# First mixture: its first two token blocks go through group 0 in two halves, fewer float64 pieces before it, and the decayed values on ScalarE

## The chip, the cores and the metric

The kernel runs on one core of a Trainium2 chip. The metric is device time in microseconds; the median of three runs of the kernel before is 2010.84 us.

The engines are named as in the profile: PE (TensorE's matmuls; PEld its weight loads), DVE (VectorE), ACT (ScalarE), POOL (GpSimd) and SP (SyncE, which issues nearly all DMAs). Each works through its own queue in program order.

## The reference, cut to what matters

```python
# retention: 4 batches x 8 heads, 576 tokens, 64 values a head
scores = scale * np.matmul(q, k.transpose(0, 1, 3, 2))
ret = scores * Dmat[None, :, :, :]          # decay gamma ** (i - j), lower triangle
x = np.matmul(ret, v)                       # -> 2304 tokens x 512

# first mixture, weights in float64: 512 -> 2048 -> 512
h = x @ w_in
g = h * (1.0 / (1.0 + np.exp(-1.702 * h)))
x = (g @ w_out).astype(np.float32)

# second mixture, eight experts, weights by a Sinkhorn iteration
for e in range(E):
    ye = np.maximum(x @ w1[e], 0.0) @ w2[e]
    out += P[:, e:e + 1] * ye
```

## The kernel before, in words

Program order is written out by hand (`manual_schedule`), so the order of calls below is the order in every engine's queue.

**Products.** Every factor of the two mixtures is kept as a high and a low part (`xh`, `xl`; `wh`, `wl`), and a product is three matmuls: high by high, high by low, low by high.

**Attention** (lines 171 to 407). Heads go two at a time: 4 head pairs by 4 batches are 16 pairs p. The 576 tokens of a pair are four chunks of 128 and a rest of 64. A loop over p = 0 to 16 works on pair p and finishes pair p - 1. SP loads `kq` (line 198, three buffers) and `aux`, the values and keys by token (line 203, four buffers), two pairs ahead. PE computes `scores` (L235, L253), DVE multiplies them by the decay (`ret`, L240, L262). `state` multiplies decayed values by keys chunk after chunk in one PSUM bank (L273); ACT copies the running sum after each chunk (L281), and the next chunk's matmuls wait for that copy. `within` (L301) and `carried` (L310) build the output; ACT (L322) and DVE (L323) evict it as `xh` and `xl`. `prep_pair` makes, a pair ahead, the decayed values `vs` (L216) and decayed queries `qs` (L223), on POOL but for the first two pairs; `qs` waits for the last `carried` of the pair whose buffer it takes, so it starts at the end of an iteration.

**Float64 pieces.** The first mixture has four groups of 512 hidden columns (`FG`). A group's weights come in 16 pieces of 128 rows by 256 columns (`HW`): 4 row chunks of `w_in` by two column halves, then 4 row chunks of `w_out` by two halves. A piece has three steps:

- `load_piece`, called by `ask`: a DMA of 256 KB from SP (L112) into one of three `raw` buffers.
- `read_piece`, called by `read`: six DVE operations (L135, L139, L140, L143, L146, L147) take the float64 bits apart into a float32 value `ca` and a rest `cs` (two buffers of each). `read` holds back two pieces that are in flight.
- `split_piece`, called by `split`: ACT writes the high part (L160), POOL subtracts it (L164) and adds the rest (L165).

`prepare` is split, ask, read, of up to three different pieces. In the attention's loop every iteration asks for one piece at its begin, splits in its middle (behind `within` 0 and 1, ahead of `state` 1) and reads at its end; after the loop what is left of group 0 is prepared at once.

**First mixture** (lines 410 to 812). 2304 tokens are blocks of 512, 512, 512, 512 and 256. For each group g and block: four calls of `mm1_chunk`, one for 128 hidden columns (12 matmuls, L429; Sigmoid on ACT, L438; product on DVE, L439; high part `gh` on ACT, L440; low part `gl` on POOL, L441; two buffers `sg`), then `mm2_first` (48 matmuls, L454, four for each f at three products each). Behind each f a hook calls `prepare` for the next group's pieces: four times in blocks 0 to 2, twice in blocks 3 and 4, 16 times a group. The result goes to `acc`: copied by ACT in group 0 (L465), added by DVE in the others (L467). Weights have two sets of buffers, `wset[g % 2]`. Eight PSUM banks go round in order.

The second mixture (behind line 812) isn't touched by the change.

Of the kernel before, what the change touches and what calls it, by code (L numbers as in the profile page):

```python
# [14 lines left out]
ALU = mybir.AluOpType  # L15
# [6 lines left out]
def retention_moe_kernel(  # L22
# [144 lines left out]
    def pieces(g):  # L167
        if g >= G1:
            return [(g, i, None) for i in range(8)]
        first = [(g, i, h) for h in range(2) for i in range(KD)]  # L170
        return first + [(g, KD + f, h) for f in range(KF) for h in range(2)]


    NC = S // P
# [36 lines left out]
    def prep_pair(p, eng):  # L211

        hp, b = pairs[p]
        vs[p] = ap2.tile([P, NC, 2, D], F32, tag="vs", name="vs")
        qs[p] = ap2.tile([P, S - P], F32, tag="qs", name="qs")
        eng.tensor_tensor(  # L216
            out=vs[p].rearrange("p c j d -> p (c j) d"),
            in0=vN(p).rearrange("p c j d -> p (c j) d"),
            in1=vt[:, hp].rearrange("p c j -> p (c j)").rearrange("p (c o) -> p c o", o=1)
            .to_broadcast([P, 2 * NC, D]),  # L220
            op=ALU.mult,
        )
        eng.tensor_tensor(  # L223
            out=qs[p], in0=kq[p][:, 1, P:S], in1=tabs[:, hp, 2 * P + NL :], op=ALU.mult
        )
# [113 lines left out]
    def read(ahead=2):  # L339
        if flight and (len(flight) > ahead or not stages["load"]):  # L340
            x = flight.pop(0)
            read_piece(*x)
            stages["split"].append(x)

    def split():
        if stages["split"]:
            split_piece(*stages["split"].pop(0))

    def prepare():
        split()  # L350
        ask()
        read()
# [15 lines left out]
    nc.sync.dma_start(out=sel_sb, in_=sel)  # L368
    nc.sync.dma_start(out=wg[:, :, 0:E], in_=w_gate.rearrange("(k p) e -> p k e", p=P))

    stages["load"] = pieces(0)
    for p in range(NP + 1):
        if p + 2 < NP:
            load_kq(p + 2)
            load_aux(p + 2)
        if p + 1 < HP:
            load_tab(p + 1)
        ask()
        if p == 0:
            scores(p)  # L380
            scores_last(p)
            for c in range(NC - 1):
                state(p, c)
            prep_pair(p + 1, nc.vector)
            continue
        if p < NP:
            scores(p)
            state(p, 0)
        state(p - 1, 3)
        within(p - 1, 0)  # L390
        within(p - 1, 1)
        split()
        if p < NP:
            state(p, 1)
            scores_last(p)
        if p < NP - 1:
            prep_pair(p + 1, nc.gpsimd)
        carried(p - 1, 1)
        if p < NP:
            state(p, 2)  # L400
        for c in (2, 3, 4):
            within(p - 1, c)
        for c in (2, 3, 4):
            carried(p - 1, c)
        read()
    while stages["load"] or stages["split"] or flight:
        prepare()
    att.close()


# [8 lines left out]
    gh = g1.tile([P, KF, 512], F32R, name="gh")  # L419
    gl = g1.tile([P, KF, 512], F32R, name="gl")  # L420

    def mm1_chunk(g, bi, f):
        t0, n = blocks[bi]
        wh, wl = wset[g % 2][0], wset[g % 2][1]
        t = bank()
        fs = slice(f * P, (f + 1) * P)
        for d in range(KD):
            for a, x in ((wh, xh), (wh, xl), (wl, xh)):
                nc.tensor.matmul(  # L429
                    out=t[:, 0:n],  # L430
                    lhsT=a[:, d, fs],
                    rhs=x[:, d, t0 : t0 + n],
                    start=d == 0 and a is wh and x is xh,
                    stop=d == KD - 1 and a is wl,
                )
        sg = g1.tile([P, 512], F32, tag="sg", name="sg", bufs=2)
        gf = sg
        nc.scalar.activation(out=sg[:, 0:n], in_=t[:, 0:n], func=ACTF.Sigmoid, scale=1.702)  # L438
        nc.vector.tensor_tensor(out=gf[:, 0:n], in0=t[:, 0:n], in1=sg[:, 0:n], op=ALU.mult)  # L439
        nc.scalar.activation(out=gh[:, f, 0:n], in_=gf[:, 0:n], func=ACTF.Copy)  # L440
        nc.gpsimd.tensor_tensor(  # L441
            out=gl[:, f, 0:n], in0=gf[:, 0:n], in1=r32(gh[:, f, 0:n]), op=ALU.subtract
        )

    def mm2_first(g, bi, hook):

        t0, n = blocks[bi]
        wh, wl = wset[g % 2][2], wset[g % 2][3]
        po = [bank() for _ in range(KD)]
        for f in range(KF):  # L450
            for d in range(KD):
                ds_ = slice(d * P, (d + 1) * P)
                for a, x in ((wh, gh), (wh, gl), (wl, gh)):
                    nc.tensor.matmul(  # L454
                        out=po[d][:, 0:n],
                        lhsT=a[:, f, ds_],
                        rhs=x[:, f, 0:n],
                        start=f == 0 and a is wh and x is gh,
                        stop=f == KF - 1 and a is wl,
                    )  # L460
            hook()
        for d in range(KD):
            xa = xacc[:, d, t0 : t0 + n]
            if g == 0:
                nc.scalar.activation(out=xa, in_=po[d][:, 0:n], func=ACTF.Copy)  # L465
            else:
                nc.vector.tensor_tensor(out=xa, in0=po[d][:, 0:n], in1=xa, op=ALU.add)  # L467
# [299 lines left out]
    for g in range(G1):  # L767
        last = g == G1 - 1
        if last:
            while stages["load"] or stages["split"] or flight:  # L770
                prepare()
            first.close()
            raw2.append(
                second.enter_context(
                    tc.tile_pool(name="raw2", bufs=1, side="right", reuse_waits="tile")
                )
            )
            begun = weight_tasks(1, True)
            tasks += weight_tasks(0) + begun[0]
        else:  # L780
            stages["load"] = pieces(g + 1)
        for bi in range(NB):
            if last and bi == 2:
                tasks += token_tasks(0, (X1K, T2, T1, X1L, T3, X2L, T4))
            for f in range(KF):
                mm1_chunk(g, bi, f)
                if pend and f >= 1:
                    pend.pop(0)()
                if last:
                    task()  # L790

            share = iter((1, 1, 1, 1) if bi < 3 else (1, 0, 1, 0))

            def hook(share=share):
                if next(share):
                    prepare()

            if last and bi == NB - 1:
                tasks += begun[1]
            mm2_first(g, bi, task if last else hook)  # L800
            if last:
                lt = []

                def a(bi=bi, lt=lt):
                    lt.append(g1.tile([P, 512], F32, tag="sg", name="lt", bufs=2))
                    gate(bi, lt[0])

                def b(bi=bi, lt=lt):
                    gate_back(bi, lt[0])

                pend += [a, b]
# [262 lines left out]
```

## Time and profile before

| | us |
|---|---|
| three runs | 2009.83, 2010.84, 2010.90 |
| median | 2010.84 |
| span of the profiled execution | 2008.7 |
| PE busy in it | 1974.4 (98%) |
| DVE busy | 1276.2 (64%) |
| POOL busy | 1197.8 (60%) |
| ACT busy | 719.9 (36%) |

The profile is one execution; it gives its span, from its first to its last instruction, and no whole time of its own. The whole times are those of the three runs, 1.1 to 2.2 us above the span.

How to read it: a timeline has the start, the duration and the engine, then line, operation, what it writes and reads, and in brackets how long the engine sat idle before it and what ended that. A chain of waits follows the work back from the last instruction. A window shows the busy time of each engine in a stretch, the granted PE clock (1.00 is 2.4 GHz) and the DMA share. On DVE and ACT an instruction can start a little before the one before it has ended.

### The profile page before, as it was taken

To read this page: it belongs to the slowest core of one execution; us is meant where nothing else is said; L and a number is where in the kernel's file an instruction comes from. 1 tells how busy PE (TensorE), PEld (TensorE's weight loads), DVE (VectorE), ACT (ScalarE), POOL (GpSimd) and SP (SyncE) were. 2 spreads that over 40 slices of the span, in tenths; PEclk is the share of its full clock that TensorE was granted. 3 is DMA by queue.
4 is the path that set the end of the run, shared out by engine and by line. 5 is a ranking of instruction groups with operands and counts; after the bars stand their busy time and mean duration, and the time that the engine had idled before them with its cause. 6 is when DMAs were issued, how large, how long until landed. Compare 5 with 4: busy or idle time off the path is not lost.

```text
span 2008.7 us, 27854 instructions
## 1 busy us (share of the span) xinstructions
PE 1974.4 (98%) x10664; PEld 1747.9 (87%) x10664; DVE 1276.2 (64%) x2189; ACT 719.9 (36%) x1459; POOL 1197.8 (60%) x1204
## 2 busy tenths in 40 slices
PE   7899999999999999999999999999999999999998
PEld 6688888877889999999999998999999998999997
DVE  6956778724676676655656667655565555555555
ACT  2343222233443333333443334333343333333332
POOL 4644545543466666666666666666666666665662
PEclk9999999999999999999999999999999999999999
DMA  8511111100212222112232222122122212122221
GB/s 317 178 37 43 43 43 43 48 22 4 71 63 63 64 80 68 64 63 79 69 95 64 70 78 63 63 66 82 63 68 90 84 64 63 64 83 65 63 63 53
DMA packets 102198, 143.92 MB, mean 72 GB/s; under 512 B 5808, under 2 KB 64944, under 8 KB 102064
## 3 DMA queue, kind: packets, MB, share of 16 engines
q1 hardware_dynamic: 101920, 142.12, 21.7%
q8 instruction: 83, 1.36, 0.3%
q14 instruction: 51, 0.42, 0.1%
q10 hardware_dynamic: 144, 0.02, 0.0%
HBM read 137.40 MB, written 4.72 MB: 71 GB/s over the span
## 4 chain that ended last, share of the span: by engine, by line
PE 91%; issue 3%; POOL 3%; DVE 2%; ACT 1%; DMA 1%; SPq 0%; POOLq 0%; ACTq 0%; DVEq 0%
PE ps_m L877 37%; PE ps_y L847 14%; PE ps L429 10%; PE ps_x L847 9%; PE ps_z L847 9%; PE ps L454 9%; POOL wi L611 1%; POOL s L585 1%; DVE cs L139 1%; PE ps L301 1%; PE ps L310 0%; DVE ca L143 0%; POOL wo L611 0%; DMA tabs<-in_tab_dram 0%; DVE ca L140 0%
## 5 line engine op out<-in xcount | busy, mean ns | idle before, releaser
L877 PE MATMUL ps_m<-wo,wo 128*128 128x512 f32 x3456 | 806.2, 391 | 4.9 <-ACT acc L888 1.5
L877 PEld LDWEIGHTS ps_m<-wo,wo 128*128 128x128 f32 x3456 | 646.3, 188 | 139.3 <-DVE acc L890 2.3
L899 DVE SCALAR_TENSOR_TENSOR acc<-ps_m,pr,acc 128x512 f32<-128x512 f32 x540 | 399.7, 748 | 233.2 <-PE ps_m L877 232.3
L611 POOL TENSOR_TENSOR wi<-r,wi 128x512 fp32r<-128x512 f32 x192 | 196.1, 1022 | 505.0 <-ACT wi L604 505.0
L857 ACT ACTIVATE wo<-u 128x384 fp32r<-128x384 f32 x192 | 100.8, 525 | 694.9 <-DVE u L990 581.8
L847 PE MATMUL ps_y<-xh,wi 128*128 128x384 f32 x1152 | 325.9, 336 | 0.8 <-DVE u L989 0.8
L611 POOL TENSOR_TENSOR wo<-r,wo 128x512 fp32r<-128x512 f32 x192 | 251.1, 1308 | 7.3 <-ACT wo L604 7.3
L611 POOL TENSOR_TENSOR wi<-s,wi 128x512 fp32r<-128x512 f32 x192 | 252.1, 1313 | 1.5 <-ACT wi L604 1.5
L847 PE MATMUL ps_z<-xh,wi 128*128 128x384 f32 x768 | 226.0, 334 | 2.4 <-DVE u L995 2.4
L847 PE MATMUL ps_x<-xh,wi 128*128 128x384 f32 x768 | 225.9, 334 | 0.0
L847 PEld LDWEIGHTS ps_y<-xh,wi 128*128 128x128 f32 x1152 | 210.8, 188 | 5.0 <-DVE u L989 1.1
L441 POOL TENSOR_TENSOR gl<-sg,gh 128x512 fp32r<-128x512 f32 (+1 forms) x80 | 95.6, 1195 | 173.3 <-ACT gh L440 135.1
L847 PE MATMUL ps_y<-xl,wi 128*128 128x384 f32 x576 | 193.1, 335 | 0.0
L861 DVE SCALAR_TENSOR_TENSOR wo<-u,wo 128x384 fp32r<-128x384 f32 x192 | 107.2, 558 | 127.0 <-ACT wo L857 127.0
L429 PE MATMUL ps<-xh,wi 128*128 128x512 f32 (+1 forms) x640 | 186.4, 370 | 0.0
L454 PE MATMUL ps<-gh,wo 128*128 128x512 f32 (+1 forms) x640 | 184.2, 368 | 0.3
L604 ACT ACTIVATE wi<-s 128x512 fp32r<-128x512 f32 x192 | 120.3, 626 | 172.8 <-POOL s L585 172.8
L585 POOL TENSOR_TENSOR s<-r 128x256 f32<-128x256 f32 x192 | 138.5, 742 | 12.2 <-DMA r<-in_w_dram 4.9
L847 PEld LDWEIGHTS ps_z<-xh,wi 128*128 128x128 f32 x768 | 141.4, 188 | 2.9 <-DVE u L995 2.9
L847 PEld LDWEIGHTS ps_x<-xh,wi 128*128 128x128 f32 x768 | 141.4, 188 | 0.0
L429 PEld LDWEIGHTS ps<-xh,wi 128*128 128x128 f32 x640 | 116.5, 188 | 23.5 <-issue 3.4
L454 PEld LDWEIGHTS ps<-gh,wo 128*128 128x128 f32 x640 | 116.2, 189 | 21.0 <-POOL wo L165 1.1
(109 smaller groups left out, 2727.1 us busy)
## 6 DMA issues: line engine op xcount, KB each, us to landing
r<-in_w_dram SPq DMA_DIRECT2D x192, 512.0 KB, 4.5
aux<-in_vk_dram SPq DMA_DIRECT2D x16, 544.0 KB, 6.4
kq<-in_kqT_dram SPq DMA_DIRECT2D x15, 576.0 KB, 4.8
raw<-in_w_in_dram SPq DMA_DIRECT2D x32, 256.0 KB, 2.6
raw<-in_w_out_dram SPq DMA_DIRECT2D x32, 256.0 KB, 2.5
out_dram<-acc SPq DMA_DIRECT2D x18, 256.0 KB, 2.6
tabs<-in_tab_dram SPq DMA_DIRECT2D x3, 384.0 KB, 7.8
kq<-in_kqT_dram SPq DMA_DIRECT2D x1, 320.0 KB, 4.1
```

The costliest lines, as they stand in the source:

```text
L139: v.tensor_scalar(out=s, in0=hi, scalar1=0x7FFFFFFF, scalar2=None, op0=ALU.bitwise_and)
L429: nc.tensor.matmul(out=t[:, 0:n], lhsT=a[:, d, fs], rhs=x[:, d, t0 : t0 + n], start=d == 0 and a is wh and x is xh, stop=d == KD - 1 and a ...
L441: nc.gpsimd.tensor_tensor(out=gl[:, f, 0:n], in0=gf[:, 0:n], in1=r32(gh[:, f, 0:n]), op=ALU.subtract)
L454: nc.tensor.matmul(out=po[d][:, 0:n], lhsT=a[:, f, ds_], rhs=x[:, f, 0:n], start=f == 0 and a is wh and x is gh, stop=f == KF - 1 and a is wl,
L585: nc.gpsimd.tensor_tensor(out=ss[:, (o - S1) % 2], in0=a, in1=b, op=op)
L604: nc.scalar.activation(out=wh, in_=t, func=ACTF.Copy)
L611: nc.gpsimd.tensor_tensor(out=wl[:, ks], in0=t[:, ks], in1=r32(wh[:, ks]), op=ALU.subtract)
L847: nc.tensor.matmul(out=t[:, 0:N], lhsT=w[:, hw, o, c], rhs=xq(q, x, hx, c), start=begin and c == 0 and i == 0, stop=end and c == 1 and i == 2,
L857: nc.scalar.activation(out=act(s, b, t)[0], in_=c, func=ACTF.Relu)
L861: nc.vector.scalar_tensor_tensor(out=l, in0=c, scalar=0.0, in1=r32(h), op0=ALU.max, op1=ALU.subtract)
L877: nc.tensor.matmul(out=t, lhsT=x[:, is_], rhs=w[:, h, f], start=f == 0 and k == 0, stop=f == 1 and k == 2,)
L899: nc.vector.scalar_tensor_tensor(out=oa, in0=tv, scalar=pr[:, ti, e : e + 1], in1=oa, op0=ALU.mult, op1=ALU.add)
```

## The change

It has four parts.

- The attention asks for pieces at p = 3 to 12 only (`EARLY = 8`); `split` goes from the middle of an iteration to its end, ahead of `read`, and the loop that prepared the rest of group 0 behind the attention is gone.
- Group 0's pieces come in another order: column half 0 of `w_in` and row chunks 0 and 1 of `w_out`, then the other half of each. Blocks 0 and 1 go through the first halves together (hidden chunks 0 and 1 of both blocks, then both output products over these), then through the second; the second output product of each is added to `acc` by DVE.
- The pieces of group 0 that are left, and group 1's behind them, are prepared in the mixture: `need` calls `prepare` until a piece that the next matmuls use has been split. Blocks 0 and 1 of group 0 have 12 calls of `prepare`, and block 3 of later groups four instead of two.
- `vs` is made by eight ACT activations of 128x64 with a scale per partition, instead of one POOL (first two pairs: DVE) product.

```diff
     def pieces(g):
         if g >= G1:
             return [(g, i, None) for i in range(8)]
-        first = [(g, i, h) for h in range(2) for i in range(KD)]
-        return first + [(g, KD + f, h) for f in range(KF) for h in range(2)]
+        first = [[(g, i, h) for i in range(KD)] for h in range(2)]
+        second = [(g, KD + f, h) for f in range(KF) for h in range(2)]
+        if g:
+            return first[0] + first[1] + second
+        return first[0] + second[:KF] + first[1] + second[KF:]
...
-        eng.tensor_tensor(
-            out=vs[p].rearrange("p c j d -> p (c j) d"),
-            in0=vN(p).rearrange("p c j d -> p (c j) d"),
-            in1=vt[:, hp].rearrange("p c j -> p (c j)").rearrange("p (c o) -> p c o", o=1)
-            .to_broadcast([P, 2 * NC, D]),
-            op=ALU.mult,
-        )
+        for c in range(NC):
+            for j in range(2):
+                nc.scalar.activation(
+                    out=vs[p][:, c, j, :],
+                    in_=vN(p)[:, c, j, :],
+                    func=ACTF.Copy,
+                    scale=vt[:, hp, c, j : j + 1],
+                )
...
+    ready = set()
+
     def split():
         if stages["split"]:
-            split_piece(*stages["split"].pop(0))
+            x = stages["split"].pop(0)
+            split_piece(*x)
+            ready.add(x)
+
+    def need(g, i, h):
+        while (g, i, h) not in ready:
+            prepare()
...
+    EARLY = 8
     stages["load"] = pieces(0)
     for p in range(NP + 1):
...
-        ask()
+        if 3 <= p < 5 + EARLY:
+            ask()
...
         within(p - 1, 1)
-        split()
...
             carried(p - 1, c)
+        split()
         read()
-    while stages["load"] or stages["split"] or flight:
-        prepare()
...
-    def mm1_chunk(g, bi, f):
+    def mm1_chunk(g, bi, f, slot=None):
         t0, n = blocks[bi]
+        slot = f if slot is None else slot
+        for i in range(KD):
+            need(g, i, f * P // HW)
...
-    def mm2_first(g, bi, hook):
+    def mm2_first(g, bi, hook, fs=range(KF), slot=0):
...
-        for f in range(KF):
+        for f in fs:
+            for h in range(2):
+                need(g, KD + f, h)
+            j = f - fs[0] + slot
...
-            if g == 0:
+            if g == 0 and fs[0] == 0:
                 nc.scalar.activation(out=xa, in_=po[d][:, 0:n], func=ACTF.Copy)
...
-            stages["load"] = pieces(g + 1)
-        for bi in range(NB):
+            stages["load"] += pieces(g + 1)
+        done = 0
+        if g == 0:
+            done = 2
+            for fs in (range(0, KF // 2), range(KF // 2, KF)):
+                for bi in range(done):
+                    for f in fs:
+                        mm1_chunk(g, bi, f, 2 * bi + f - fs[0])
+                    prepare()
+                for bi in range(done):
+                    mm2_first(g, bi, prepare, fs, 2 * bi)
+        for bi in range(done, NB):
...
-            share = iter((1, 1, 1, 1) if bi < 3 else (1, 0, 1, 0))
+            share = iter((1, 1, 1, 1) if bi < 3 or g and bi < 4 else (1, 0, 1, 0))
```

Where the listing leaves lines out, `mm1_chunk` and `mm2_first` use `gh` and `gl` at `slot` and `j` instead of `f`, and a product starts and stops at the first and last f of `fs`.

## Rows read from the trace of the kernel before

**Rows 1.** The chain that ended last: shares of the span by engine

```profile
PE 91%; issue 3%; POOL 3%; DVE 2%; ACT 1%; DMA 1%; SPq 0%; POOLq 0%; ACTq 0%; DVEq 0%
```

**Rows 2.** Window of the attention: stretch, busy by engine (instructions), clock, DMA share, GB/s

```profile
17.20:92.57 75.37, 60.70 (x1053) 49.68 (x1049) 68.14 (x154) 25.80 (x100) 50.48 (x53) 1.00 0.71 255
```

**Rows 3.** The chain in order of time, attention: start, us, what

```profile
21.40 0.45 ACT xh L322
...
80.61 1.14 DVE cs L139
...
82.90 0.21 ACT st L281
...
84.80 0.45 ACT xh L322
...
92.57 0.43 PE ps L429
```

**Rows 4.** Timeline of PE, early attention: the scores of two pairs in turn

```profile
17.20 1.16 PE L235 MATMUL ps<-kq 64*128 64x128 f32 x16
...
21.28 1.16 PE L235 MATMUL ps<-kq 64*128 64x128 f32 x16
```

**Rows 5.** Timeline of POOL, one iteration of the attention

```profile
50.99 0.85 POOL L164 TENSOR_TENSOR ca<-ca,wi 128x256 f32<-128x256 f32 x1 [1.47 <-ACT wi L160]
...
53.60 1.27 POOL L223 TENSOR_TENSOR qs<-kq,tabs 128x448 f32<-128x448 f32 x1
```

**Rows 6.** Timeline of DVE, the same iteration and the attention's last but one

```profile
51.17 1.28 DVE L240 TENSOR_TENSOR ret<-ps,tabs 128x512 f32<-128x512 f32 x2
...
53.59 0.28 DVE L135 TENSOR_SCALAR ca<-raw 128x256 uint32<-128x256 uint32 x1
...
91.02 0.28 DVE L135 TENSOR_SCALAR ca<-raw 128x256 uint32<-128x256 uint32 x1
...
93.06 0.82 DVE L323 TENSOR_TENSOR xl<-ps,xh 128x256 fp32r<-128x256 f32 x2
```

**Rows 7.** Timeline of DVE, first mixture, groups 0 and 1

```profile
102.98 0.69 DVE L439 TENSOR_TENSOR sg<-ps,sg 128x512 f32<-128x512 f32 x1 [1.19 <-ACT sg L438]
...
182.06 0.42 DVE L439 TENSOR_TENSOR sg<-ps,sg 128x256 f32<-128x256 f32 x1 [4.33 <-ACT sg L438]
...
203.87 0.28 DVE L135 TENSOR_SCALAR ca<-raw 128x256 uint32<-128x256 uint32 x1
...
207.90 0.82 DVE L135 TENSOR_SCALAR ca<-raw 128x256 uint32<-128x256 uint32 x1
...
210.97 0.83 DVE L135 TENSOR_SCALAR ca<-raw 128x256 uint32<-128x256 uint32 x1
...
239.31 2.47 DVE L467 TENSOR_TENSOR acc<-ps,acc 128x512 f32<-128x512 f32 x4
```

**Rows 8.** Timeline of POOL, first mixture

```profile
183.01 0.74 POOL L441 TENSOR_TENSOR gl<-sg,gh 128x256 fp32r<-128x256 f32 x1 [6.81 <-PE ps L429]
...
208.65 0.87 POOL L165 TENSOR_TENSOR wo<-ca,cs 128x256 fp32r<-128x256 f32 x1
...
211.72 0.87 POOL L165 TENSOR_TENSOR wo<-ca,cs 128x256 fp32r<-128x256 f32 x1
```

**Rows 9.** The chain in order of time, group 1, block 0

```profile
191.62 10.92 PE ps L429 x48
...
212.65 1.20 PE ps L454 x4
```

**Rows 10.** Timeline of ACT, attention: two state copies behind each other

```profile
18.74 0.34 ACT L281 ACTIVATE st<-ps 128x64 f32<-128x64 f32 x2 [0.98 <-PE ps L273]
```

**Rows 11.** Loads of aux in the attention, all sixteen

```profile
DMA to landing us min/median/max: 4.5/6.4/8.5
```

**Rows 12.** Timeline of PE, and a window, at the kernel's start

```profile
9.22 0.48 PE L273 MATMUL ps<-vs,aux 128*64 128x64 f32 x4 [2.59 <-DVE vs L216]
...
10.20:13.60 3.40, 2.90 (x26) 2.30 (x28) 2.70 (x6) 0.45 (x2) 0.00 (x0) 0.50 1.06 395
```

More of the change, by code (lines that the diff above doesn't have):

```diff
@@ L439, in mm1_chunk @@
         nc.vector.tensor_tensor(out=gf[:, 0:n], in0=t[:, 0:n], in1=sg[:, 0:n], op=ALU.mult)
-        nc.scalar.activation(out=gh[:, f, 0:n], in_=gf[:, 0:n], func=ACTF.Copy)
+        nc.scalar.activation(out=gh[:, slot, 0:n], in_=gf[:, 0:n], func=ACTF.Copy)
         nc.gpsimd.tensor_tensor(
-            out=gl[:, f, 0:n], in0=gf[:, 0:n], in1=r32(gh[:, f, 0:n]), op=ALU.subtract
+            out=gl[:, slot, 0:n], in0=gf[:, 0:n], in1=r32(gh[:, slot, 0:n]), op=ALU.subtract
         )
-    def mm2_first(g, bi, hook):
+    def mm2_first(g, bi, hook, fs=range(KF), slot=0):
         t0, n = blocks[bi]
@@ L456, in mm2_first @@
                         lhsT=a[:, f, ds_],
-                        rhs=x[:, f, 0:n],
-                        start=f == 0 and a is wh and x is gh,
-                        stop=f == KF - 1 and a is wl,
+                        rhs=x[:, j, 0:n],
+                        start=f == fs[0] and a is wh and x is gh,
+                        stop=f == fs[-1] and a is wl,
                     )
```

## The prediction

> **What bounds the kernel now.** Read first the chain that ended last: PE has 91% of it [rows 1]; time is won only where PE waits. The stages are then read in order. In the attention PE is busy 60.7 of 75.4 us [rows 2], so this stage has slack. Later PE is full almost without a gap: whatever makes PE wait there is a loss at full price.
>
> The attention's period is 5.34 us, twelve iterations from the ScalarE eviction at 21.40 to the one at 84.80 of which the first, with no split yet, was shorter. The chain [rows 3] shows the ring: VectorE reads a float64 piece, its L139 held to 1.14 us; ScalarE's L160, queued ahead of the state copy L281, waits for that read; PE's L273 waits for L281; the eviction at the iteration's end waits for PE; VectorE's next read waits for that. Before the first piece is read PE runs an iteration without a gap, 17.20 to 21.28, **4.08 us** [rows 4]. L139 is long because GpSimd's L223 (53.60 to 54.87 in another iteration [rows 5]) runs beside it. A read that meets nothing takes 2.04 us, 91.02 to 93.06 [rows 6].
>
> The first mixture hides its reads behind 10.9 us runs of 48 matmuls, but not always: with GpSimd splitting beside it a read takes 3.07 us (207.90 to 210.97), and the one that follows a GELU 4.03 us (203.87 to 207.90) [rows 7]. In group 1, block 0, two reads are left over; PE's last four matmuls, 1.20 us, start at 212.65, when the last split ends at 212.59 [rows 8, 9]. Its 48 matmuls take 11.3 us from 202.54 to 213.85 instead of 10.9: PE already waits 0.4 us, and the cover is used up.
>
> **Part 1, the attention.** Asks run at p = 3 to 12 only: ten asks, eight reads (end of p = 5 to 12), eight splits (end of p = 6 to 13). Removed are eight of sixteen asks in the loop with their SP issues, seven reads in the loop and two after it, and the splits that go with them. Splitting moves from the middle of an iteration to its end, past GpSimd's L223 and ScalarE's last eviction, ahead of the next read. L160 then takes a piece read one iteration earlier, so the ring is cut.
>
> Without a read an iteration is 4.08 us. With one, VectorE's own sum is the limit. From its first score product to the next read is 2.42 us, 51.17 to 53.59 [rows 6], of which I estimate 0.3 us as the wait for the last eviction, part of the ring; with an undisturbed read 2.04 + 2.12 = 4.2 us. GpSimd now runs L223, L164 and L165 in one burst, 1.27 + 0.85 + 0.87 = 3.0 us [rows 5, 8], just when the read begins. If they collide as badly as today it stays at 5.34 us. I take **4.7 us**, the middle, because VectorE can fall about 1.5 us behind PE (PE needs the scores' product only behind the next scores, 1.16 us [rows 4]), by when most of the burst is past. That lead is used up before PE waits: 8 x 0.62 - 1.5 = 3.5 us over the floor. After 21.40: 13 x 4.08 = 53.0 to the last eviction but one, 3.5, and the tail, 92.57 - 84.80 - 5.34 = 2.4: the attention ends at 80.4 instead of 92.57. **-12.2 us**; bounds -15.7 (floor) and -5.6 (5.34 in eight iterations).
>
> The values on ScalarE (L216): eight 128x64 activations replace one GpSimd product, which lay on no path of the chain. No row has one with a scale per partition; the nearest are state copies of the same size, two in 0.34 us, so 0.12 us more for each further one and 0.22 alone [rows 10]: 1.0 us, at most 1.8. They stand ahead of an eviction, a state copy and the last eviction, all on ScalarE; it waited 0.98 us for PE before those copies [rows 10] and as long ahead of the last eviction, so the cost is nothing unless they wait for aux. Its load takes 6.4 us in the median and 8.5 at most [rows 11]; from its issue at the end of p-1 to its use in p+1 (for pair p+2) there are 0.6 + 4.08 + 2.1 = 6.8 us (end of that iteration, one iteration, ScalarE's place in the next). A late one would hold the state copy that PE waits for; up to 1 us of it is covered. Price 0 to 1 us an iteration; it is inside the two bounds above.
>
> **Part 2, the first two blocks of group 0.** The matmuls are the same; every second half adds four VectorE sums of 0.62 us (2.47 for four [rows 7]) a block, which lie beside matmuls. But twelve reads now go through VectorE in these 43.5 us, against eight in the stretch of the same length before. Count from the first matmul, chunks of 2.72 us: chunks of the first half end at 10.88, its output products at 21.76, chunks of the second half at 32.64. VectorE leaves the last GELU of the first half 1.3 us after its chunk, at 12.2 (203.87 is 1.3 behind the chunk that ended at 202.54 [rows 7, 9]). Five reads follow in program order (pieces 9 to 13): 4.03 + 4 x 3.07 = 16.3, to 28.5. Only then the GELUs of the second half, two by two, one read after each pair. Late GELUs follow each other by 1.88 us, 0.69 + 1.19 [rows 7]. So GELUs at 28.5 and 30.4, piece 14 from 31.0 to 35.0, GELUs at 35.0 and 36.9, piece 15 from 37.6. A read after a GELU has its split ended 5.65 us after it began (203.87 to 209.52 [rows 7, 8]): 43.2. PE has some 1.1 us of matmuls behind it [rows 9]: the block's products end near 44.1 instead of 38.1. PE loses **+6.0 us**, the first part behind piece 14, whose L160 stands on ScalarE behind the GELU of the last chunk. Bounds 2 (GELUs on time: piece 15 from 33.9, split at 39.5) and 7.
>
> In that wait PE does 0.5 us of work in about 6. At the start it sat idle for 2.59 us before 9.22, and in 10.2 to 13.6 the granted clock was 0.50, that is 1.2 GHz [rows 12]. I reckon with a fall here too: about 2.8 us of the matmuls behind the wait at half rate, **+1.4 us**; bounds 0 and 3.4. The Trainium skill, "TensorE: Matmul & The Clock Gate", section "HAM oscillation — how this bites in real kernels", says that waits which idle PE bring the clock back to half; the rows of the start agree. By it the fall is certain; by a stage like the attention (PE busy four fifths, clock 1.00 [rows 2]) it would not come and the sum would be 1.4 less.
>
> At the begin two small waits go (the mixture's first GELUs now meet a ScalarE free for its table): -0.3.
>
> **Part 3, later groups.** Group 0 now makes 20 calls of prepare for six leftover pieces plus sixteen of group 1. At its end eleven of those are split, twelve read; thirteen and fourteen before. So four reads instead of two fall into group 1's first output product. Two more at 3.07 us, behind a cover already used up: **+6.1 us**; bounds 4 and 7. Group 2's begins with all but one split done: -0.4.
>
> To catch up, block 3 of groups 1 and 2 takes four reads instead of two. VectorE then reaches the sums at 1.3 + 4.03 + 3 x 3.07 = 14.5 us after the block's output product began, and block 4's first GELU 2.4 later, at 17.0. Block 4 has 256 tokens, a little over half of 10.9 us a run, so PE is there at 10.9 + 5.7 = 16.6. From GELU to its low half takes 1.69 us (182.06 to 183.75 [rows 7, 8]): 18.6 where the second matmul wants it at 16.7. **+1.9 us, twice: +3.8**; bounds 0 and 5.
>
> **Sum.** -12.2 + 6.0 + 1.4 - 0.3 + 6.1 - 0.4 + 3.8 = **+4.4 us**. The profiled execution has a span of 2008.7 us; the runs are 2009.83 to 2010.90, so 1.1 to 2.2 lie around it, and the change is set against the median: 2010.84 + 4.4 = **2015.2 us**. From 0.2%, 4.0 us, a measurement can tell a difference, so the forecast, slower, stands right at that line.
>
> **Rivals.** *The attention at PE's floor.* If the burst is past when VectorE reads, -15.7 holds; with the clock kept at 1.00 the sum is -15.7 + 6.0 - 0.3 + 6.1 - 0.4 + 3.8 = -0.5: 2010.3. For it: the lag of VectorE makes room by itself. Against: the burst is 3.0 us long.
>
> *Faster: the second half's reads do not run late.* Place: pieces 9 to 15 in the first two blocks. If reads there go nearer 2.04 than 3.07, because the splits are done before the next read comes, VectorE is at the GELUs when PE is and the 6.0 is at most 1. It decides as soon as five reads take under 13 us. With the floor in the attention: -0.5 - 5.0 = -5.5, 2005.3; were group 1's four reads quicker too, more. Against: read follows read at 3.07 wherever splits run.
>
> *The attention wins little.* The lock between VectorE and GpSimd: the read meets L223, then L164, then L165, and iterations stay near 5.34; -5.6 instead of -12.2: +11.0, 2021.8. For it: the row of L139. The Trainium skill, "SBUF — State Buffer", section "Who interferes with whom", says that of a VectorE and a GpSimd instruction needing their shared port pair the later waits for the whole of the earlier. The row of L139 agrees: 1.14 us, to the end of L223.
>
> That the change fails to take pieces out of the attention can be left aside: the order of asks is written out.
>
> **How the numbers follow.** The forecast has 0.50, on its own range 2011 to 2019, which the 4.0 us line cuts: 0.28 slower, 0.21 same, 0.01 faster. The floor has 0.22 (0.21 same), the quicker reads 0.14 (faster), the small win 0.14 (slower). Faster 0.16, same 0.42, slower 0.42. The range from 2005.5 to 2020.5 leaves out about half each of the two outer rivals and holds the bounds of the forecast's terms taken together.
>
> **What would show it.** Right: L273 no longer waits for L281 behind L160; reading iterations of 4.2 to 5.2, the first mixture starting near 80; PE waits of 5 to 6 us behind L160 and L165 (piece 14, 15) about 35 us into the mixture, some 6 us behind L165 in group 1's first output product, about 2 us behind L441 in block 4 of groups 1 and 2, and a granted clock under 1.00 after the first of these. Wrong: the mixture starting later than 87 or before 77.5, the first wait absent, or waits in blocks not named here.

## The result, and the profile after

The kernel after takes 2023.95 us in the median of four runs (2018.66 to 2024.78), the kernel before 2010.87 beside it: a ratio of 1.0055 (95% interval 1.0040 to 1.0069), slower by 0.55%. That is outside the range. Three of the four executions agree within 1.4 us, the fourth is 5 us shorter. The profiled execution took 2023.44 us; its span is 2021.6 against 2008.7, 12.9 us more. In the tables below a stretch runs from the first hidden-layer matmul of one block to that of another:

| stretch | before | after | difference | forecast |
|---|---|---|---|---|
| start of the span to the first mixture | 92.5 | 84.7 | -7.8 | -12.2 |
| group 0, blocks 0 and 1 | 43.9 | 51.2 | +7.3 | +7.1 |
| group 0, blocks 2 to 4 | 55.0 | 55.0 | 0 | 0 |
| group 1, block 0 | 22.2 | 28.3 | +6.1 | +6.1 |
| group 1, block 4 | 11.5 | 15.4 | +3.9 | +1.9 |
| group 2, block 0 | 22.2 | 21.8 | -0.4 | -0.4 |
| group 2, block 4 | 11.5 | 15.4 | +3.9 | +1.9 |

They add up to +13.0; all that is left out agrees within 0.1 us. Two terms failed, the attention by 4.4 us and block 4 by 2.0 in each of two groups. The chain that ended last has less of PE than in [rows 1], and VectorE has 8% of it instead of 2%:

```profile
PE 83%; DVE 8%; issue 4%; POOL 3%; ACT 1%; DMA 1%; SPq 0%; POOLq 0%; ACTq 0%
```

**The attention.** Answering to [rows 12, 4], the start on ScalarE, then PE (start, duration, line, and in brackets the idle time and its releaser):

```profile
9.71 1.28 ACT L221 ACT_TABLE_LOAD   x1 [9.71 <-DMA aux<-in_vk_dram]
11.00 2.02 ACT L221 ACTIVATE vs<-aux,vt 128x64 f32<-128x64 f32 x8
```

```profile
11.40 0.72 PE L277 MATMUL ps<-vs,aux 128*64 128x64 f32 x4 [4.21 <-ACT vs L221]
```

The first pair's values stand on the path: ScalarE's table is loaded only when `aux` has come, and the eight activations take 2.02 us, not 1.0. The scores that were at 17.20 [rows 4] are at 19.76, a loss of 2.6 us. From there six iterations take 4.04, then seven reading ones 4.50, 4.43, 4.42, 5.63, 5.62, 4.04 and 5.53, 4.88 in the mean. The late ones begin so (the chain, then ScalarE, then SP's waits from 45 to 75 us: in total, times, longest):

```profile
49.92 7.25 DMA aux<-in_vk_dram
...
63.41 1.24 DVE cs L147
```

```profile
57.54 2.02 ACT L221 ACTIVATE vs<-aux,vt 128x64 f32<-128x64 f32 x8 [1.78 <-DMA aux<-in_vk_dram]
```

```profile
SPq L112 <- DVE cs L147: 19.8, 6, 4.6
```

The ask for a piece waits for VectorE's last read of the buffer that it takes; `kq` and `aux` stand behind it on SP's queue. `aux` lands 7.25 us after its issue, ScalarE stands 1.78 us, and from then on GpSimd's `qs` meets VectorE's L147 (1.24 us instead of 0.43).

**The first two blocks.** VectorE's GELUs (L454, the product with the sigmoid) and reads (L135 begins one) of the second half, then PE's waits, GpSimd's last step of pieces 14 and 15, and two windows (stretch, busy by engine, clock, DMA share, GB/s):

```profile
113.62 0.68 DVE L454 TENSOR_TENSOR sg<-ps,sg 128x512 f32<-128x512 f32 x1
115.49 0.69 DVE L454 TENSOR_TENSOR sg<-ps,sg 128x512 f32<-128x512 f32 x1 [1.18 <-ACT sg L453]
116.10 0.40 DVE L135 TENSOR_SCALAR ca<-raw 128x256 uint32<-128x256 uint32 x1
...
120.11 0.68 DVE L454 TENSOR_TENSOR sg<-ps,sg 128x512 f32<-128x512 f32 x1
...
122.58 0.37 DVE L135 TENSOR_SCALAR ca<-raw 128x256 uint32<-128x256 uint32 x1
```

```profile
119.96 0.73 PE L472 MATMUL ps<-gh,wo 128*128 128x512 f32 x2 [0.32 <-POOL wo L165]
123.69 0.80 PE L472 MATMUL ps<-gh,wo 128*128 128x512 f32 x1 [2.53 <-ACT wo L160]
126.41 1.22 PE L472 MATMUL ps<-gh,wo 128*128 128x512 f32 x2 [1.50 <-POOL wo L165]
```

```profile
125.63 0.72 POOL L165 TENSOR_TENSOR wo<-ca,cs 128x256 fp32r<-128x256 f32 x1
...
127.30 0.86 POOL L165 TENSOR_TENSOR wo<-ca,cs 128x256 fp32r<-128x256 f32 x1
```

```profile
124.00:128.00 4.00, 2.50 (x6) 1.50 (x6) 3.93 (x6) 0.42 (x1) 3.84 (x5) 0.50 0.06 9
128.00:132.00 4.00, 4.00 (x15) 3.19 (x14) 3.83 (x8) 0.42 (x1) 1.88 (x3) 0.75 0.38 122
```

From the mixture's start these GELUs stand at 28.9, 30.8 and 35.4 us, where 28.5, 30.4 and 35.0 were forecast. The three waits are for piece 13's low part, then for piece 14's high part and its low part (done at 126.35); piece 15's low part is done at 128.16, about 1 us before PE needs it. In group 1's block 0 PE waits for L165 five times, 4.2 us in the brackets; one of the five (a bracket counts from the modelled end of the matmul before, 0.39 us after its start, where in a full run the next starts after 0.23: so it understates what a wait costs):

```profile
212.08 0.73 PE L472 MATMUL ps<-gh,wo 128*128 128x512 f32 x2 [1.13 <-POOL wo L165]
```

**Block 4.** VectorE's sums after the four reads, PE's waits, and the window behind:

```profile
288.59 2.48 DVE L485 TENSOR_TENSOR acc<-ps,acc 128x512 f32<-128x512 f32 x4
290.98 0.42 DVE L454 TENSOR_TENSOR sg<-ps,sg 128x256 f32<-128x256 f32 x1
```

```profile
291.90 0.38 PE L472 MATMUL ps<-gh,wo 128*128 128x256 f32 x1 [1.48 <-ACT gh L455]
292.71 0.39 PE L472 MATMUL ps<-gl,wo 128*128 128x256 f32 x1 [0.42 <-POOL gl L456]
```

```profile
294.00:298.00 4.00, 4.00 (x23) 4.00 (x23) 3.38 (x7) 1.62 (x5) 3.19 (x5) 0.60 0.00 0
```

The brackets of the two waits add up to the 1.9 us of the forecast; what they cost is 2.4 (run 1 below). The granted clock of 0.60, much of the stretch at 1.2 GHz, was not in the forecast.

### The profile page after: what moved, and what is told of

It reads as the page before. It is cut to its first block, busy times and chain, and to the rows that moved or that the text cites. A ratio compares the mean times of both kernels' runs of the same rounds, so it can differ in the third digit from the quotient of the medians.

```text
span 2021.6 us, 27964 instructions
## 1 busy us (share of the span) xinstructions
PE 1983.7 (98%) x10664; PEld 1753.4 (87%) x10664; DVE 1282.7 (63%) x2195; ACT 747.5 (37%) x1587; POOL 1182.9 (59%) x1190
## 3 DMA queue, kind: packets, MB, share of 16 engines
q1 hardware_dynamic: 101920, 142.12, 21.8%
## 4 chain that ended last, share of the span: by engine, by line
PE 83%; DVE 8%; issue 4%; POOL 3%; ACT 1%; DMA 1%; SPq 0%; POOLq 0%; ACTq 0%
PE ps_m L905 37%; PE ps_y L875 14%; PE ps_x L875 9%; PE ps_z L875 9%; PE ps L444 6%; PE ps L472 5%; DVE ca L143 1%; DVE ca L140 1%; POOL wi L629 1%; DVE ca L135 1%; DVE sg L454 1%; POOL s L603 1%; DVE cs L146 1%; DMA aux<-in_vk_dram 1%; ACT sg L453 1%
## 5 line engine op out<-in xcount | busy, mean ns | idle before, releaser
L472 PE MATMUL ps<-gh,wo 128*128 128x512 f32 (+1 forms) x640 | 190.7, 377 | 11.5 <-POOL wo L165 6.0
```

What stands on the lines that cost most here:

```text
L472: nc.tensor.matmul(out=po[d][:, 0:n], lhsT=a[:, f, ds_], rhs=x[:, j, 0:n], start=f == fs[0] and a is wh and x is gh, stop=f == fs[-1] and ...
```

## The experiments

The ratio behind each time is to the kernel before as it ran in the same session. Its medians there were 2011.50 us (runs 1 to 3 and 8), 2013.13 (5 to 7 and 9), 2012.91 (4, 10 and 11) and 2012.14 (12), so runs of different sessions compare by their ratios. Starts, stages and iterations are those of one profiled execution of each. From the first mixture's last block on, in code that only run 9 touches, the granted clock fell once in the profiles of runs 1, 2, 4, 11 and 12, and that stretch took 1.2 to 1.8 us more than in the kernels before and after; in run 6 it fell twice, 2.9 to 3.1 us more. Differences of that size between whole times need not come from an edit. Code is shortened.

**1. The first two pairs' values back on VectorE.** In the kernel after:

```diff
+        if p < 2:  eng.tensor_tensor(vs[p], vN(p), vt)   # as before the change
+        else:      eight nc.scalar.activation(...)
```

> The changed kernel, with the decayed values of the first two pairs back on VectorE; ScalarE makes them from the third pair on. Theory (the start costs 2.6 us, because ScalarE's table load now stands behind the first aux, and the first state product behind eight activations of 0.25 us): the first mixture starts near 82.2 us instead of 84.8, and the time is 2.6 us lower, near 2021.4. Rival (the loads of the first pairs set the pace, so the 2.6 us come back as a later wait for aux): no gain, 2024.

2020.20 us, 1.0041 (1.0026 to 1.0056). The scores of p = 2 are at 17.15, the mixture starts at 80.6: 4.1 us won, 2.6 of them at the start, as the theory has it; the other 1.5, which it had not, because one iteration is long (5.53) instead of three.

**2. All values back.** In the kernel after `prep_pair` is as before the change.

```diff
-                nc.scalar.activation(...)        # eight a pair
+        eng.tensor_tensor(out=vs[p], in0=vN(p), in1=vt, op=ALU.mult)
```

> The changed kernel, with all decayed values back where they were (VectorE for two pairs, GpSimd for the rest). Theory (ScalarE's in-order wait for a late aux holds PE in the last reading iterations, some 3 us): besides the 2.6 us of the start that wait goes too, mixture start near 79, total 5 to 6 us lower, 2018 to 2019. Rival (the lock: GpSimd's burst beside the read grows from 3.0 to 4.0 us and reading iterations go to 5 us or more): not under 2021.

2026.09 us, 1.0067 (1.0050 to 1.0084); the mixture starts at 87.2, with iterations up to 7.6 us (the two longest have a fall of the granted clock in them, 0.66 in the mean from 45 to 50 us and from 72 to 77). The rival held: VectorE and GpSimd lock each other out. VectorE, then GpSimd:

```profile
52.55 1.02 DVE L146 TENSOR_SCALAR cs<-ca 128x256 uint32<-128x256 uint32 x1
53.60 1.25 DVE L147 SCALAR_TENSOR_TENSOR cs<-raw,cs 128x256 f32<-128x256 uint32 x1
```

```profile
52.20 1.22 POOL L219 TENSOR_TENSOR vs<-aux,vt 128x512 f32<-128x512 f32 x1
53.44 1.14 POOL L226 TENSOR_TENSOR qs<-kq,tabs 128x448 f32<-128x448 f32 x1
```

L146 ends with `vs` (53.57 and 53.42), L147 with `qs` (54.85 and 54.58); alone they take 0.29 and 0.43.

**3. The split moved, nothing else.** In the kernel before:

```diff
         within(p - 1, 1)
-        split()
...
+        split()
         read()
```

> The kernel before, with one thing changed: split at the end of an attention iteration, ahead of read, as in the changed kernel. All sixteen pieces stay in the attention and the mixture is as before. Theory (it is the ring through L160 and the state copy that makes 5.34 us, and the change gains by cutting it, not by having fewer pieces): iterations of 4.5 to 4.9 us, mixture start at 83 to 87 instead of 92.6, and no loss behind it: 2001 to 2005. Rival (VectorE's reads against GpSimd's burst bound it, fewer pieces are what pays): iterations stay near 5.3 us, 2009 to 2011.

2012.39 us, 1.0002 (0.9992 to 1.0011). The mixture starts at 93.3; iterations go from 4.4 to 6.7. L140 takes 1.27 us beside `vs`, L146 1.27 beside `qs`:

```profile
49.85 1.27 DVE L140 SCALAR_TENSOR_TENSOR ca<-raw,ca 128x256 uint32<-128x256 uint32 x1
...
51.61 1.27 DVE L146 TENSOR_SCALAR cs<-ca 128x256 uint32<-128x256 uint32 x1
```

```profile
49.77 1.06 POOL L216 TENSOR_TENSOR vs<-aux,vt 128x512 f32<-128x512 f32 x1 [0.91 <-PE ps L253]
51.59 1.14 POOL L223 TENSOR_TENSOR qs<-kq,tabs 128x448 f32<-128x448 f32 x1 [0.76 <-PE ps L310]
```

The theory fell. The ring is cut, for from 40 to 66 us the chain is VectorE's work and short issue alone; with the values on GpSimd the lock gives about the same length.

**4. Only the values moved.** The kernel before, pairs 2 and up on ScalarE, split in the middle:

> The kernel before with one edit: the decayed values of pairs 2 and up on ScalarE. The split stays in the middle of the iteration, ahead of a state copy. Theory (the ring and the lock are two bounds of about the same height; the ring alone still gives 5.3 us, since VectorE's read is held by GpSimd's qs as before and the split still waits for that read): iterations of 5.2 to 5.4 us, the first mixture starting at 91 to 93 us, 2008 to 2012 us. Rival (the values on GpSimd were the whole of what held the attention, and moving the split adds nothing): iterations of 4.8 us or less in the mean as in the run with all pieces and both edits, the mixture starting at 87 to 88 us, 2005 to 2008 us.

2007.42 us, 0.9977 (0.9967 to 0.9987): faster than before. Iterations are a steady 4.88 us from the third reading one on, the mixture starts at 88.0. The theory's 5.3 fell; the rival's time came, and runs 5 and 6, which move the split as well, are not faster than this one. The ring is still there, now through ScalarE: the chain goes from the read by way of L160 and the state copy to the eight values, the eviction of `xh` and the next read.

```profile
63.89 0.42 ACT L160 ACTIVATE wo<-ca 128x256 fp32r<-128x256 f32 x1 [0.91 <-DVE ca L143]
64.22 0.20 ACT L291 ACTIVATE st<-ps 128x64 f32<-128x64 f32 x1
64.32 2.01 ACT L227 ACTIVATE vs<-aux,vt 128x64 f32<-128x64 f32 x8
66.23 0.36 ACT L332 ACTIVATE xh<-ps 128x256 fp32r<-128x256 f32 x1
```

**5. Both, all sixteen pieces in the attention**, the mixture as before:

> The kernel before, all sixteen pieces in the attention and the mixture untouched, with only two edits: the split moved to the end of the iteration, and the decayed values of pairs 2 and up on ScalarE (the first two pairs as before). Theory (the attention's ring and the lock between VectorE and GpSimd were both real, each hides the other, and only both edits together cut them; the losses behind the attention come from the moved reads alone): reading iterations of 4.4 to 4.6 us where aux is in time and up to 5.6 where it is late, the first mixture starting at 81 to 88 us instead of 92.6, the mixture's stages as long as before (start to block 2 44.0, group 1 block 0 22.2), 2000 to 2006 us. Rival (with a piece in every iteration, aux is late in all of them and holds 5.3 to 5.6 us): the mixture starting at 91 to 94, 2009 to 2013 us.

2008.34 us (2005.42 to 2013.18), 0.9980 (0.9969 to 0.9991). The mixture starts at 87.0, its stages are as long as before: within the theory's 81 to 88 for the start, above its 2006 in the median. Most reading iterations go 4.0 to 4.4 and 5.5 to 5.6 in turn, a mean of 4.9. The profiled execution was the fastest of the seven, 2005.42.

**6. As 5, with four float64 buffers.**

```diff
-    rawp = ...tile_pool(name="rawp", bufs=3, side="right")
+    rawp = ...tile_pool(name="rawp", bufs=4, side="right")
```

> As the run with all pieces and both edits, and the float64 pieces have four buffers instead of three. Theory (aux comes late because the ask for a piece stands ahead of kq and aux on SP's queue and waits there until VectorE has read the piece whose buffer it takes): with a fourth buffer the ask finds a free one, aux lands in time, reading iterations of 4.4 to 4.6 us throughout, the first mixture starting at 81 to 83 us, 1999 to 2002 us. Rival (aux is late for the size of its transfer and the order on the queue, not for the ask's wait): the same as with three buffers within 1 us.

2006.85 us, 0.9972 (0.9963 to 0.9981), not to be told from 5; the mixture starts at 87.8. ScalarE no longer waits for `aux` at all from 35 to 85 us, but the alternation stays. So the theory was right on `aux` and wrong on the time: late `aux` was not what held these iterations. What did, VectorE and GpSimd in a long one:

```profile
64.60 1.38 DVE L147 SCALAR_TENSOR_TENSOR cs<-raw,cs 128x256 f32<-128x256 uint32 x1
```

```profile
64.56 1.14 POOL L233 TENSOR_TENSOR qs<-kq,tabs 128x448 f32<-128x448 f32 x1 [1.27 <-PE ps L320]
```

`qs` starts 0.04 us ahead of L147, which then takes 1.38; PE waits for VectorE's `ret` behind it. In run 12 L147 is 0.11 ahead, `qs` waits instead, and the iteration is 4.42:

```profile
59.74 0.43 DVE L147 SCALAR_TENSOR_TENSOR cs<-raw,cs 128x256 f32<-128x256 uint32 x1
```

```profile
59.85 1.31 POOL L236 TENSOR_TENSOR qs<-kq,tabs 128x448 f32<-128x448 f32 x1 [1.62 <-PE ps L323]
```

The pieces read beside a `qs` in the kernel after and in runs 5, 6, 7, 10 and 12 agree: where `qs` starts first, by 0.02 to 0.26 us, L147 takes 1.24 to 1.39, and where L147 starts first it takes 0.42 to 0.43. What makes the one or the other come first isn't shown.

**7. As 1, with four float64 buffers.**

> The kernel after with the values of the first two pairs back on VectorE, and a fourth buffer for float64 pieces. Theory: the last late iteration of the run with the first values on VectorE (5.53 us) goes too and the mixture starts at 79.5 to 80.0 instead of 80.7; the losses of 7.3, 6.1, 3.9 and 3.4 us behind the attention stay, 2018.5 to 2020.5 us, still slower than before: the attention alone cannot pay for the moved reads. Rival (the fourth buffer also lets pieces land ahead in the first two blocks of group 0, and the waits there shrink): 2012 to 2016 us.

2018.57 us, 1.0032 (1.0022 to 1.0042); the mixture starts at 80.2, eight pieces read at 4.4 each but for one of 5.3. The losses behind stay: 51.6 us for the first two blocks, 28.3 for group 1's block 0. The theory held, but for the one long iteration.

**8. The catch-up moved by a block.** In the kernel after, block 4 of groups 1 and 2 takes the four reads, block 3 two as before the change:

```diff
-            share = iter((1, 1, 1, 1) if bi < 3 or g and bi < 4 else (1, 0, 1, 0))
+            share = iter((1, 1, 1, 1) if bi < 3 or g and bi > 3 else (1, 0, 1, 0))
```

> The changed kernel, but in groups 1 and 2 block 3 prepares two pieces and block 4 four, instead of four and two. Theory (block 4's short first product can't hide block 3's four reads: 1.9 us of wait each and about 1.6 us of lower clock behind it): both waits go, and with them 6 to 7 us: 2017 to 2018. Rival (the reads are then late for the next group's first block, and the wait only moves): 2022 to 2024.

2017.96 us, 1.0031 (1.0019 to 1.0043). Block 4 is back at 11.5 in both groups, with no fall of the clock; the next group's block 0 gives back 0.9 (22.7 instead of 21.8). The theory held: twice 3.9 less twice 0.9 are 6.0 us.

**9. PE kept busy in block 4's wait.** In the kernel after, ahead of the output product of block 4 in groups 1 to 3 (in group 3, which the expectation leaves out, PE has no such wait):

```diff
+            for _ in range(13):
+                nc.tensor.matmul(out=po[0][:, 0:n], lhsT=wh[:, 0, 0:P], rhs=xh[:, 0, t0 : t0 + n], ...)
```

> The kernel after, and ahead of the output product of block 4 in groups 1 and 2 thirteen matmuls of 256 columns more, whose result is overwritten, in the bank that the product takes next. They add some 1.4 us of work to PE just where it waits 1.5 us for the first GELU. Theory (behind that wait the clock's fall costs 1.7 us in each group, over the wait itself): no window at the granted clock of about 0.6 behind block 4, each of the two groups shorter by 1.0 to 1.7 us, 2020 to 2022 us where the kernel after has 2023.9. Rival (the clock falls for another reason, or its records mean nothing for the time): the low windows stay, or go without a gain, 2023 to 2025 us.

2020.94 us, 1.0040 (1.0025 to 1.0055), an interval that overlaps that of the kernel after (1.0040 to 1.0069). Block 4 takes 13.9 us in groups 1 and 2 instead of 15.4, and the window is at full clock:

```profile
294.00:298.00 4.00, 3.58 (x30) 3.46 (x30) 2.45 (x7) 2.11 (x6) 2.66 (x4) 1.00 0.00 0
```

What the fall costs is shown by run 1, where group 1's block 4 took 13.9 us and group 2's 15.4, behind waits of 1.41 and 1.44: 1.5 us are the clock's, 2.4 are the wait's (1.9 in the two brackets). That the added matmuls kept the clock up isn't shown, because in runs 7 and 10 it stayed up without them in both groups, behind waits of 1.44 to 1.49 us. One of these, in run 10, and the window behind it:

```profile
281.38 0.38 PE L481 MATMUL ps<-gh,wo 128*128 128x256 f32 x1 [1.49 <-ACT gh L464]
```

```profile
283.00:287.00 4.00, 4.00 (x36) 4.00 (x35) 3.14 (x8) 1.84 (x5) 3.04 (x5) 1.00 0.01 4
```

Of ten such places, in the kernel after and runs 1, 2, 7 and 10, four have the fall.

**10. Twelve pieces early.** As 7, with four pieces more in the attention:

```diff
-    EARLY = 8
+    EARLY = 12
```

> The kernel after with the values of the first two pairs on VectorE and four float64 buffers (as the run with both), and twelve asks' worth more pieces in the attention: EARLY is 12, so twelve pieces of group 0 are read there and four are left. Theory (all that is lost behind the attention comes from reads moved into stages without room; the two halves themselves cost nothing): four more reading iterations cost 4 x 0.4 to 1.5 us, the mixture starts at 82 to 86 us; start to block 2 takes 44.0 to 45 us instead of 51.6, group 1's block 0 22 to 23 instead of 28.3; block 4 of groups 1 and 2 keeps its 2.4 us (or 3.9 where the clock falls), since block 3 still takes four reads; 2009 to 2013 us. Rival (the halves cost by themselves, by the sums into acc or by the order on ScalarE): the stretch from the start to block 2 stays above 48 us, 2014 us or more.

2015.68 us, 1.0015 (1.0006 to 1.0025). The profiled execution was the fastest of the ten, 2010.04; where the median one lost 5.6 us more isn't shown. In the profile the attention did better than expected, a steady 4.42 us and the mixture at 80.5; group 1's block 0 took 21.8. But blocks 0 and 1 still took 49.6 and block 2 23.5: against before again 7.4 us, now mostly in one wait of PE, ahead of block 2:

```profile
130.15 0.78 PE L453 MATMUL ps<-xh,wi 128*128 128x512 f32 x1 [5.06 <-DVE acc L494]
```

The rival's mark of 48 us was passed. VectorE's sums L494 stand behind the reads, twelve of them still: a call of `prepare` that finds group 0 done reads a piece of group 1.

**11. As 10, with block 3's old share.**

```diff
-            share = iter((1, 1, 1, 1) if bi < 3 or g and bi < 4 else (1, 0, 1, 0))
+            share = iter((1, 1, 1, 1) if bi < 3 else (1, 0, 1, 0))
```

> As the run with twelve early pieces, and block 3 of groups 1 and 2 takes two reads as before the change. Theory (with twelve pieces read early, group 1 is ready in time, so the four reads in block 3 only bring the wait in block 4): block 4 of groups 1 and 2 at 11.5 us as before the change, block 0 of group 2 at 21.8 to 22.7, some 4 to 5 us less than with the four reads: 2004 to 2008 us, as good as all sixteen pieces in the attention. Rival (the reads taken out of block 3 are missing in front of the next group's block 0): block 4 gains 2.4 us and block 0 of the next group loses as much, no change within 1 us.

2009.34 us, 0.9985 (0.9976 to 0.9994). Block 4 takes 11.5 us, block 0 of group 2 22.2. The theory held for these stages; the time is 1.3 us above its range, and blocks 0 to 2 still take 7.8 us more than before.

**12. As 11, with eight reads in the first two blocks.**

```diff
                         mm1_chunk(g, bi, f, 2 * bi + f - fs[0])
-                    prepare()
...
+            (1, 1, 1, 0) if g == 0 and bi == 3   # a third call of prepare there
```

> As the run with twelve early pieces and the old share, but the first two blocks of group 0 have eight calls of prepare instead of twelve (those between the hidden chunks go), and block 3 of group 0 three instead of two. Theory (the 7.4 us there are lost because twelve reads in that stretch are more than VectorE can do there, whichever group's pieces they are; the twelve early pieces left that count as it was, so the loss stayed): with eight reads the sums into acc come in time, start to block 2 takes 44 to 46 us and block 2 21.8 to 23 instead of 49.7 and 23.8, group 1's block 0 22 to 23; 2001 to 2005 us, faster than every kernel so far. Rival (the second half's sums on VectorE, 0.6 us each and eight of them, or the halves' order, cost by themselves): start to block 2 stays above 48 us or block 2 above 23.5, 2007 to 2010 us.

2003.99 us, 0.9961 (0.9947 to 0.9975): the lowest median here, 0.4% under before, with an interval that overlaps those of runs 4 to 6. Blocks 0 and 1 take 44.6 and block 2 21.8; PE's one wait there, of 0.67 us, is for L165. The mixture starts at 81.5. Group 1's block 0 takes 25.2, not 22 to 23: two waits of 1.1 are left. So without the four calls blocks 0 to 2 take 7.1 us less than in run 11, and 3.4 of them come back in group 1's block 0. The halves cost 0.7 us at most. The four calls were also those between the hidden chunks, ahead of the GELUs, so whether it was the number of reads or their place isn't told apart.

## Why the prediction was wrong

The sign was forecast, the size was not: +4.4 against +12.9 in the spans. Of the 8.5 us between them the start has 2.6, the iterations 1.8, and block 4 of groups 1 and 2 twice 2.0: 1.5 for a fall of the clock and 0.5 for a longer wait.

**The attention, -12.2 forecast, -7.8 measured.** Two of its terms failed, the price of the values and the length of a reading iteration.

- "the nearest are state copies of the same size [...] 1.0 us, at most 1.8": it is 2.0. They follow each other by 0.24 us and one takes 0.34, against 0.12 and 0.22 taken from the state copies [rows 10]. Those have no scale per partition. The Trainium skill, "ScalarE: Activation LUTs", section "What ACT_TABLE_LOAD costs", adds some 93 ns for a pointer operand to 186 ns and 0.833 ns an element, and lets neighbours overlap by as much. An estimate from these figures of that page is 0.33 us alone and 0.24 in a row for 64 elements, and the trace agrees.
- "so the cost is nothing unless they wait for aux" overlooked the first pair. No earlier work covers it, and PE waits 4.21 us for it. Price 2.6 us; run 1 gives it back.
- "I take **4.7 us**, the middle", less a lead of VectorE of 1.5 us in all: the thirteen iterations have 5.4 us over 13 x 4.08 instead of the 3.5 forecast. The seven that read have 4.88 in the mean, made of 4.0 to 4.5 and of 5.5 to 5.6 by the order of `qs` and L147; that the mean lies near 4.7 is luck.

A third reading was wrong, though it is no part of the 4.4 us: "one GpSimd product, which lay on no path of the chain". Taking it off GpSimd was worth more than moving the split. Run 3 moves the split alone and wins nothing, run 4 moves the values alone and wins 0.46 us an iteration (5.34 to 4.88), both together bring 4.42 where the order of two engines falls well, and about 4.9 in the mean where it does not (runs 5 and 6). A chain shows one bound; the lock stood behind it at the same height.

The late `aux`, "Price 0 to 1 us an iteration", was seen and came: 1.78, 0.49 and 0.86 us. It was put down to the transfer; in the kernel after it is the ask ahead of it, held by VectorE for up to 4.6 us. Runs 6 and 7 take it away with a fourth buffer; the mixture then starts 0.5 us earlier in run 7 than in run 1 and 0.8 later in run 6 than in run 5, one execution of each.

**The first two blocks, +6.0, +1.4 and -0.3 forecast, +7.3 measured.** The sum is right and its first steps are: GELUs within 0.5 us of the times worked out, the long wait for piece 14's L160, the clock at 0.50 behind it. The last step is not. PE was to wait for piece 15's L165; the second long wait is for piece 14's, and PE at half clock comes to piece 15 later than it is done. By an estimate from the starts of the matmuls (0.43 us apart instead of 0.23 from 124 to 130 us) the clock cost about 2 us and the waits about 5, where 1.4 and 6.0 were forecast: that they make up for each other is luck. Runs 11 and 12 show which calls mattered: four of the twelve, whichever group's.

**Group 1, block 0, +6.1 forecast and measured**: two reads more at 3.07 us; run 12 has one read more than before there, and 3.0 us. **Group 2, block 0**: -0.4 as forecast.

**Block 4, +3.8 forecast, +7.8 measured.** The waits were placed rightly and sized a little short (1.9 forecast, 2.4 measured). The failed step is that the clock's fall was reckoned for the wait in the first two blocks only, and here put at nothing: 1.5 us a group were missing. Run 8 takes wait and fall away.

**The rivals.** "The attention wins little" gave 2021.8, the nearest; its lock is real, but what decides is the order of `qs` and L147, and iterations did not stay at 5.34. "Faster: the second half's reads do not run late" fell: five reads took 16.3 us as reckoned (97.31 to 113.62), not under 13. The range's upper end, 2020.5, had nothing for the start (2.6) or the clock at block 4 (twice 1.5); with these 5.6 us the result would lie inside. Nor did it hold "the bounds of the forecast's terms taken together": the upper ones, -5.6, 7, 3.4, 7 and 5 beside -0.3 and -0.4, add up to +16.1, which is 2026.9.

## What to carry to other kernels

Work that moves to a fuller stage should be counted as calls in a stretch, on the engine that does them: the loss in the first two blocks stayed when pieces of group 0 were taken out and others came in their place (run 10), and went when calls were taken out (run 12), half of it to the next stretch. An engine's product that lies on no chain can still hold another engine, so cutting one of two bounds of the same height can win nothing (run 3). A short wait on a full PE can carry a fall of the clock (1.5 us on top of 2.4 in block 4), and the first pass of a loop is costed by itself, since nothing covers it. Moving the values alone (run 4, 0.9977) isn't told apart from the lowest of all (run 12, 0.9961): the halves and the fewer early pieces have shown no gain of their own.

## What was not expected of the hardware

- Of VectorE and GpSimd whoever starts first holds the other, and 0.04 or 0.11 us decide between iterations of 5.5 and 4.4 us. VectorE's products of 512 columns that read PSUM (`ret`) took 0.67 to 0.69 in every iteration of the kernel before, the kernel after and runs 2, 3, 6 and 7. The Trainium skill, "SBUF — State Buffer", section "Who interferes with whom", puts it as order of issue, for a VectorE instruction with two SBUF inputs or in a mode that uses the shared port pair too, which it says `tensor_scalar` can enter; the rows of L147 (two inputs) and of L146 and L139 (`tensor_scalar`, 1.02 and 1.14 us) agree.
- The granted clock fell to 1.2 GHz behind waits of 1.44 and 0.42 us, and did not behind 1.41 and 0.42 in the same execution (run 1), nor behind 1.49 and 0.42 in run 10: the length of the waits alone does not decide.
